# Row-tiled attention scores, early sums weighed later, whole-tile weight splits and a new issue plan in a fused attention, mixture-of-experts and squared-ReLU kernel

## The chip, the cores and the metric

One NeuronCore of a Trainium2 chip runs the whole kernel. The metric is device time in microseconds for one execution; a kernel is judged by the median of several runs. Beside them one execution was recorded by the profiler; its rows are what is read below. The engines are TensorE (PE for matmuls, PEld for the loads of their stationary operand), VectorE (DVE), ScalarE (ACT), GpSimd (POOL) and SyncE (SP), which issues most of the transfers.

## The reference

Three stages, all in f32 at the interface, on 4 batches of 576 positions, 8 heads of 64:

```python
# 1 attention with a causal window of 128 and a linear bias per head
scores = scale * q @ k.T            # per head
scores = where(0 <= rel < 128, scores - slope[h] * rel, -1e9)
attn = exp(scores - max); attn = attn / (sum + 1e-9);  x = attn @ v   # 2304 x 512
# 2 eight experts, every token to every expert, weights P by 8 row/column scalings
P = exp(x @ w_gate - max); 8 times: rows to 1, columns to 1, P *= N / E
out = sum over e of P[:, e] * (relu(x @ w1[e]) @ w2[e])               # 512 -> 1024 -> 512
# 3 squared ReLU layer
y = (relu(out @ w_in) ** 2) @ w_out                                   # 512 -> 2048 -> 512
```

## The kernel before

**Products.** The layers of stages 2 and 3 are done in 40 runs (e, b): experts e = 0 to 7 by batches b, then the two halves of the last layer (e = 8 and 9) by batches. Every operand is held as a high and a low f16 part and every product is three matmuls (THREE, L39). Each 2 x 2 block product is a seven-product scheme (m1 to m7, L44), so operands need sums of quarters and results are sums of products. A run is 336 matmuls of 128 x 128 by 288 columns: 168 for the hidden layer (`hidden`), 168 for the second one (`layer`). ScalarE or VectorE evict each product from PSUM into a quarter of a tile q (`to_quarter`), and cast hidden values to high and low (`split`).

**Attention.** 16 pairs of heads (two heads a and a + 1 on the two halves of the partitions), four units u of 128 queries each. `score_ops` (L856) writes the scores of a unit for both heads into one PSUM bank: a bf16 matmul of the identity by the bias tile first, then matmuls of Q by K onto it. For the first two batches (WHOLE = 2) Q is an f32 tile in which the other head's half is zero, so that a matmul contracts over 128 partitions. For the others `make_heads` (L823) casts Q and K to high and low f16 parts. `unit` (L881) takes the maxima from PSUM (VectorE), scales them, takes exp with its sum (ScalarE), scales by the reciprocal, transposes on TensorE and moves the result. `values` multiplies by V in f32. `take_x` and `take_sums` make the operands x of the batch, and expert 0 starts on a batch as soon as these are there, so attention of later batches and runs of expert 0 share the engines.

**Gate and early sums.** P needs all four batches, so runs that end before P is known (EARLY, five of them) are written to DRAM as they are (`spill`). `weigh` (L1146) starts when P is there: it brings each one back, multiplies by P (`by_p`, VectorE) and writes or adds it to acc_s in DRAM. A later run's sum q may be added (`y_next`, L1181) only when its batch has been weighed. `convert` (L1268) turns the last layer's 32 weight pieces, which come as 64-bit floats, to f32 and f16 parts, from the end of the weighing on, in the order of all of win and then wout. `retake` and `operands` read acc_s back and make the last layer's operands.

**Weights.** `Weights.make` (L563) splits a staged tile of 128 x 1024 in two halves k, each in a piece of 3 quarters ahead of the sums (`combine_w`) and one of 4 behind.

**What sets the order.** The program is written out by a planner (`Sched`) when it is built. Each chain of work is a thread; the planner knows a modelled cost of every operation and of every transfer (BEGIN, moves, LANDS, STORED, ADDED), and issues next the operation whose modelled start, less a lead, is earliest. Leads are constants (LEAD_...) or grow as a due time counted in products comes near (`by`, L387, with SLOPE, FAR and MARGIN). Where two engines can do an operation (`either`, `move`) the prices in PRICE choose. On each engine, and on the queues that issue transfers, the order so written is kept; an engine waits at whatever is next.

Of the kernel before, what the change touches and what calls it, by code (L numbers as in the profile page):

```python
# [86 lines left out]
LEAD_ATT, LEAD_LOGIT, LEAD_W0, LEAD_GATE, LEAD_WEIGH = -0.2988, -0.1623, -0.5925, -0.2787, 0.2666  # L87
SLOPE, FAR = 0.0083, 35.3894
MARGIN = {'TAKE': 8.6326, 'TAKE2': 8.6184, 'SPLIT': 0.7677, 'ADD': 10.9442, 'W': 4.7897, 'CONV': -22.9922, 'RETAKE': -15.7173}

AGE = 0.206

PRICE = {'A': -0.074, 'D': 0.577, 'G': 0.181, 'GW': 0.465, 'GS': 0.613, 'DF': 0.694, 'DR': 0.417, 'DM': 0.123, 'DN': 0.55, 'DX': 0.486, 'AS': -0.04, 'T': 0.0, 'S': 0.0}

SPARE = 6
WHOLE = 2


FRONT = dict(zip("PQRSTX", (((0,), 1), ((1,), 1), ((2,), 1), ((0, 1, 3, 4), 4), ((2, 5, 6), 3), ((7,), 1))))
MIDDLE = dict(zip("PQRSTX", (((0,), 1), ((1,), 1), ((2,), 1), ((3, 4), 2), ((5, 6), 2), ((7,), 1))))  # L100
# [9 lines left out]
RATE = {"A": 0.83e-3, "D": 1.04e-3, "G": 2.1e-3}  # L110
# [4 lines left out]
BEGIN, LANDS, STORED, ADDED = 0.65, 1.15, 0.35, 3.2  # L115
# [5 lines left out]
class Op:  # L121


    def __init__(self, engine, cost, reads, writes, issue, moves=0.0, lands=0.0, double=False):
        self.engine, self.cost, self.reads, self.writes, self.issue, self.moves, self.lands = engine, cost, reads, writes, issue, moves, lands
        self.price = PRICE[engine]

        self.port = engine == "G" or (engine == "D" and (double or sum(a.space != PSUM and a.free_size() > 8 for a in reads) > 1))
# [81 lines left out]
class Sched:  # L210
# [5 lines left out]
    def __init__(self):  # L216
        self.free = dict.fromkeys("TADGS", 0.0)
        self.port = self.moved = 0.0
        self.warm = 6.0
        self.place, self.marks, self.threads, self.count = {}, {}, [], 0  # L220
# [27 lines left out]
    def issue(self, op, start):  # L248
        op.issue()
# [29 lines left out]
    def run(self, until=None):  # L279
        while self.threads:  # L280
# [14 lines left out]
            for th in self.threads:  # L295
# [8 lines left out]
                key = (start - th.lead() if callable(th.lead) else start - th.lead - AGE * (start - ready), th.order)  # L304
# [40 lines left out]
def attn_moe_relu2(ctx: ExitStack, tc: tile.TileContext, qT, kT, v, wg, w1, w2, win, wout, bias, out):  # L345
# [12 lines left out]
    identb = const.tile([128, 128], BF16, name="identb")  # L358
# [27 lines left out]

    def by(due, kind):  # L387

        margin = MARGIN[kind]
        return lambda: -SLOPE * min(FAR, max(-5.0, (due - state["products"]) * PRODUCT + margin))  # L390
# [43 lines left out]
    def ts(out, in0, s, op, s2=None, op2=None):  # L434
# [4 lines left out]
            "D", START["D"] + RATE["D"] * size(out) / (2 if fast else 1) + 0.06 * (len(reads) - 1), reads, [out],  # L439
            lambda: nc.vector.tensor_scalar(out, in0, s, s2, op0=op, **k), double=fast,  # L440
        )

    def stt(out, in0, s, in1, op0, op1):
        return Op(
            "D", START["D"] + RATE["D"] * size(out), [in0, in1], [out],
            lambda: nc.vector.scalar_tensor_tensor(out=out, in0=in0, scalar=s, in1=in1, op0=op0, op1=op1),  # L446
        )
# [20 lines left out]
    def mms(seq):  # L468

        cost, reads, writes = 0.0, [], []  # L470
        for o, l, r, _, _ in seq:
            n = size(o)
            cost += 0.0025 + (n / 1200 if r is None else (4 * max(n, 112) if r.dtype == F32 else max(n, 44)) / 2400)
# [30 lines left out]
    def dma(out, in_):  # L504
        m = moves(out, in_)
        return Op("S", 0.46, [in_], [out], lambda: nc.sync.dma_start(out=out, in_=in_), m, STORED if out.space == DRAM else LANDS)
# [25 lines left out]
    def priced(kind, op):  # L532
        op.price = PRICE[kind]
# [4 lines left out]
    class Weights:  # L538
# [24 lines left out]
        def make(self, kind, c, t):  # L563
# [13 lines left out]
    def products(operands, known, banks, take, order, base, due, end):  # L577
# [14 lines left out]
        for step, (m, i0, i1) in enumerate(order):  # L592
# [15 lines left out]
            state["products"] += len(seq)  # L608
            if i1 == n:
# [157 lines left out]
    state = {"logits": 0, "wgs": False, "att": False, "gate": False, "weigh": False, "run": 0, "products": 0}  # L767

    with tc.manual_schedule():
        make_identity(nc, ident)  # L770
        nc.vector.tensor_copy(identb, ident)
        nc.vector.memset(ones, 1.0)

        with ExitStack() as actx:
            apool = lambda name, bufs, **k: actx.enter_context(tc.tile_pool(name=name, bufs=bufs, **k))
            ap = apool("ap", 1)
            r_qk = ring("qk32", ap, 3, [128, 2, S])
            r_kl = ring("kl", ap, 2, [128, 2, S], F16)
            r_b = ring("bia", ap, 2, [128, 512], BF16)
            r_e = ring("e", ap, RE, [128, 4, 2, 64])  # L780
            r_et = ring("eT", ap, 2, [128, 24, 64])
            qs = [ap.tile([128, 2, S], F32, name=f"q{i}") for i in range(2)]
            vs = [ap.tile([128, 9, 2, 64], F32, name=f"v{i}") for i in range(2)]

            for t in qs:
                nc.gpsimd.memset(t[64:128, 0], 0.0)
                nc.gpsimd.memset(t[0:64, 1], 0.0)
# [3 lines left out]
            r_q2, r_v = Kept(qs), Kept(vs)  # L791
            r_xq = ring("xq", ap, RX, [128, 4, HT])
            r_nm = ring("nm", ap, RE, [128, 4])
            r_sm = ring("sm", ap, RE, [128, 4])

            pairs = [(b, p) for b in range(B) for p in (0, 2, 1, 3)]
            qk32, qk, bias_in, values_in, eT, scored, moved = {}, {}, {}, {}, {}, {}, {}

            def load_heads():
                for n, (b, p) in enumerate(pairs):  # L800
                    h = slice(2 * p, 2 * p + 2)
                    if b < WHOLE:
                        Q = yield Need(r_q2)
                        for a in range(2):
                            yield dma(Q[64 * a : 64 * a + 64, a], qT[b, 2 * p + a])
                        K = yield Need(r_qk)
                        yield dma(K[:, 0], kT[b, h].rearrange("h d s -> (h d) s"))
                        qk[b, p] = (Q, K), ((r_q2, Q), (r_qk, K))
                    else:
                        t = []  # L810
                        for src in (qT, kT):
                            x = yield Need(r_qk)
                            for i in range(2):
                                yield dma(x[64 * i : 64 * i + 64], src[b, h].rearrange("h d s -> d h s"))
                            t.append(x)
                        qk32[b, p] = t
# [3 lines left out]
                    if n == 0:  # L820
                        spawn(load_values(), LEAD_ATT)

            def make_heads():  # L823


                for at in pairs[NP * WHOLE :]:
                    yield lambda: at in qk32
                    q32, k32 = qk32.pop(at)
                    t = yield Need(r_q2)
                    x = t.rearrange("p a s -> p (a s)").bitcast(F16).rearrange("p (i a s) -> p i a s", i=2, a=2)  # L830
                    Q, KH = x[:, 0], x[:, 1]
                    KL = yield Need(r_kl)
                    yield act(Q, q32)
                    yield either(Q[64:128], q32[64:128], Q[64:128], ALU.subtract)
                    r_qk.free(q32)
                    yield act(KH, k32)
                    yield either(KL, k32, KH, ALU.subtract)
                    r_qk.free(k32)
                    qk[at] = (Q, KH, KL), ((r_q2, t), (r_kl, KL))

# [15 lines left out]
            def score_ops(at, u, ps):  # L856
                full = lambda x: x.rearrange("p (a c) -> p a c", a=2)
                f, t = full(ps), full(bias_in[at])
# [552 lines left out]
```

## Time and profile before

| | us |
|---|---|
| runs | 1883.63, 1877.82, 1883.71 (median 1883.63) |
| profiled execution, its own time | 1878.17 |
| its span | 1876.4 |
| PE busy | 1814.9 (97%) |
| PEld busy | 1445.2 (77%) |
| DVE busy | 1576.8 (84%) |
| ACT busy | 1244.3 (66%) |
| POOL busy | 169.3 (9%) |

The span is the part of the profiled execution in which instructions ran. Busy time of PE includes the modelled ends of pipelined matmuls, so neighbouring groups overlap, and the distance from one group's start to the next one's is the better measure of what a group takes. The transfers take a mean of 136 GB/s, with stretches of 253 GB/s (about 420 to 470 us) and 273 GB/s (about 1500 to 1550 us).

### The profile page before, as it was taken

To read this page: it belongs to the slowest core of one execution; us is meant where nothing else is said; L and a number is where in the kernel's file an instruction comes from. 1 tells how busy PE (TensorE), PEld (TensorE's weight loads), DVE (VectorE), ACT (ScalarE), POOL (GpSimd) and SP (SyncE) were. 2 spreads that over 40 slices of the span, in tenths; PEclk is the share of its full clock that TensorE was granted. 3 is DMA by queue.
4 is the path that set the end of the run, shared out by engine and by line. 5 is a ranking of instruction groups with operands and counts; after the bars stand their busy time and mean duration, and the time that the engine had idled before them with its cause. 6 is when DMAs were issued, how large, how long until landed. Compare 5 with 4: busy or idle time off the path is not lost.

```text
span 1876.4 us, 38768 instructions
## 1 busy us (share of the span) xinstructions
PE 1814.9 (97%) x15077; PEld 1445.2 (77%) x15077; DVE 1576.8 (84%) x3475; ACT 1244.3 (66%) x3217; POOL 169.3 (9%) x207
## 2 busy tenths in 40 slices
PE   8899999898999999999999999999999999999999
PEld 7778777686777777777777777777777777777777
DVE  7987778897799999999999999999867777666666
ACT  7998876665566666666666667666646566666555
POOL 1110001100101212110012111111000000000000
PEclk9999999998999999999999999999999999999999
DMA  6554412438655535444453555345445585121321
GB/s 164 168 141 109 138 52 74 134 117 253 178 149 151 155 101 159 141 120 118 149 162 93 149 163 164 94 133 147 112 161 146 156 273 178 70 110 63 128 102 70
DMA packets 88233, 255.44 MB, mean 136 GB/s; under 512 B 26992, under 2 KB 35312, under 8 KB 88048
## 3 DMA queue, kind: packets, MB, share of 16 engines
q1 hardware_dynamic: 79984, 219.93, 35.2%
q0 software_dynamic: 8064, 33.03, 9.9%
q8 instruction: 118, 1.93, 0.4%
q14 instruction: 67, 0.55, 0.1%
HBM read 168.57 MB, written 84.35 MB: 135 GB/s over the span
## 4 chain that ended last, share of the span: by engine, by line
PE 60%; DVE 20%; DMA 8%; ACT 7%; issue 4%; SPq 0%; POOL 0%; DVEq 0%; ACTq 0%; POOLq 0%
PE ps L482 60%; DVE h L431 5%; DVE q L431 4%; DVE t L431 3%; ACT q L414 2%; DVE w L446 2%; DMA acc_s<-q 2%; DMA wst<-in_w 2%; DMA x_s<-wo 2%; ACT h L414 1%; ACT e L414 1%; DVE wz L431 1%; DVE wo L446 1%; ACT w L414 1%; DMA yw<-y_s 1%
## 5 line engine op out<-in xcount | busy, mean ns | idle before, releaser
L482 PEld LDWEIGHTS <-w 128*128 128x128 f16 x13440 | 1315.7, 98 | 395.9 <-issue 65.0
L482 PE MATMUL ps<-x,w 128*128 128x288 f16 x6720 | 861.2, 286 | 32.9 <-ACT q L414 19.1
L482 PE MATMUL ps<-h,w 128*128 128x288 f16 x6720 | 857.4, 286 | 14.4 <-DVE q L431 5.8
L414 ACT ACTIVATE q<-ps 128x288 f32<-128x288 f32 x926 | 364.5, 403 | 279.6 <-PE ps L482 268.6
L431 DVE TENSOR_TENSOR q<-ps,q 128x288 f32<-128x288 f32 x672 | 291.5, 449 | 106.5 <-PE ps L482 85.4
L414 ACT ACTIVATE q<-q 128x288 f32<-128x288 f32 x411 | 174.9, 440 | 95.2 <-DVE q L431 93.3
L414 ACT ACTIVATE h<-t 128x576 f16<-128x576 f32 x320 | 212.6, 679 | 30.8 <-DVE t L431 28.3
L414 ACT ACTIVATE h<-q 128x288 f16<-128x288 f32 x480 | 203.8, 439 | 4.4
L414 ACT ACTIVATE w<-wst 128x384 f16<-128x384 f32 (+1 forms) x256 | 141.1, 572 | 80.0 <-DMA wst<-in_w 38.0
L431 DVE TENSOR_TENSOR h<-q,h 128x288 f16<-128x288 f32 x384 | 173.3, 465 | 24.2 <-ACT h L414 23.3
L431 DVE TENSOR_TENSOR h<-t,h 128x576 f16<-128x576 f32 x256 | 188.5, 754 | 1.8 <-ACT h L414 0.9
L446 DVE SCALAR_TENSOR_TENSOR w<-wst,w 128x384 f16<-128x384 f32 (+1 forms) x256 | 161.4, 638 | 8.7 <-ACT w L414 8.4
L431 POOL TENSOR_TENSOR wst<-wst 128x256 f32<-128x256 f32 x107 | 97.1, 909 | 585.4 <-DVE wst L431 334.0
L431 DVE TENSOR_TENSOR t<-q,t 128x288 f32<-128x288 f32 x315 | 140.5, 456 | 1.9 <-ACT q L414 1.0
L431 DVE TENSOR_TENSOR t<-q 128x576 f32<-128x576 f32 x160 | 122.8, 770 | 6.2 <-ACT q L414 4.0
L431 DVE TENSOR_TENSOR q<-q,pb 128x576 f32<-128x576 f32 x108 | 83.6, 784 | 6.3 <-ACT q L414 5.6
L510 POOL DMA_DIRECT2D acc_s<-q x54 | 47.5, 907 | 431.2 <-DVE q L431 404.8
L414 ACT ACTIVATE e<-ps,nm 128x192 f32<-128x192 f32 (+1 forms) x160 | 64.1, 410 | 15.7 <-DVE nm L440 12.7
L431 DVE TENSOR_TENSOR wst<-wst 128x256 f32<-128x256 f32 x149 | 61.8, 426 | 2.4 <-POOL wst L431 0.5
L414 ACT ACTIVATE wo<-wz 128x384 f16<-128x384 f32 x64 | 36.8, 574 | 38.4 <-DVE wz L431 17.7
L453 DVE TENSOR_REDUCE nm<-ps 128x2 f32<-128x384 f32 (+1 forms) x80 | 38.3, 495 | 18.7 <-PE ps L482 18.4
L446 DVE SCALAR_TENSOR_TENSOR h<-q,h 128x288 f16<-128x288 f32 x96 | 43.1, 450 | 12.6 <-ACT h L414 12.6
(94 smaller groups left out, 1059.3 us busy)
## 6 DMA issues: line engine op xcount, KB each, us to landing
x<-x_s SPq DMA_DIRECT2D x56, 1008.0 KB, 4.8
wst<-in_w SPq DMA_DIRECT2D x64, 512.0 KB, 4.7
acc_s<-q POOLq DMA_DIRECT2D x54, 576.0 KB, 6.8
pb<-p_s SPq DMA_DIRECT2D x32, 288.0 KB, 5.5
yw<-in_win SPq DMA_DIRECT2D x16, 512.0 KB, 5.4
yw<-in_wout SPq DMA_DIRECT2D x16, 512.0 KB, 4.9
x_s<-x SPq DMA_DIRECT2D x8, 1008.0 KB, 4.9
win_s<-wo SPq DMA_DIRECT2D x16, 448.0 KB, 3.1
```

Of the source, the lines that this page charges most:

```text
L414: return Op("A", cost, reads, writes, lambda: nc.scalar.activation(out=out, in_=in_, func=func, scale=scale, **k))
L431: lambda: engine(e).tensor_tensor(out=out, in0=in0, in1=in1, op=op),
L446: lambda: nc.vector.scalar_tensor_tensor(out=out, in0=in0, scalar=s, in1=in1, op0=op0, op1=op1),
L453: lambda: nc.vector.tensor_reduce(out=out, in_=in_, axis=axis, op=op, **k),
L482: nc.tensor.matmul(o, l, r, start=start, stop=stop, skip_group_check=True)
L510: return Op("G", 1.04, [in_, out], [out], lambda: nc.gpsimd.dma_start(out=out, in_=in_, accum_op=ALU.add), m, ADDED)
```

## The change

- **Scores.** All pairs are f32 and unpadded. Each score matmul contracts over the 64 partitions of one head, and the two heads alternate, each into a PSUM bank of its own; two units at a time share the two banks (`two` takes the place of `unit`; `make_heads`, the padded Q, the identity in bf16 and the bias matmuls go). The bias is added by VectorE while it takes the score from PSUM into e, with the minimum of the scaled sum kept beside (`add_min`); exp then reads e. Scaling e by the reciprocal may also go to GpSimd. Q and K come in one transfer each, the first K issued from ScalarE's queue.
- **Running array.** Until the first expert run starts, `fill` issues matmuls of a constant tile into an own PSUM bank wherever the planner sees TensorE free, each counted as 0.216 us.
- **Early sums.** EARLY has six runs. Whichever term of acc_s comes first is written, the others are added (`give`), in any order of runs. `weigh` takes the n-th tile at 336 (8 + 2 n) products.
- **Weights and conversion.** `Weights.make` splits both halves k in one instruction each. `convert` squares on ScalarE where VectorE masked a sign, is due over runs 13 to 35, and does the first half of win and wout first.
- **Plan.** LEAD, MARGIN, SLOPE, AGE and PRICE become entries of PLAN that change at 1000, 1900, 6000 and 9400 products. Landing times and GpSimd's rate are raised. PSUM banks of the front are dealt out anew; the second half of a batch in `operands` uses the ring of staged weights.

```diff
-LEAD_ATT, LEAD_LOGIT, LEAD_W0, LEAD_GATE, LEAD_WEIGH = -0.2988, -0.1623, -0.5925, -0.2787, 0.2666
-SLOPE, FAR = 0.0083, 35.3894
...
+PLAN = [
+    (0, {
+        "ATT": -0.2046, "LOGIT": -0.3502, "W0": -0.4909, "GATE": 0.3571, "CAST": -0.315, "SLOPE": 0.015925,
...
-FRONT = dict(zip("PQRSTX", (((0,), 1), ((1,), 1), ((2,), 1), ((0, 1, 3, 4), 4), ((2, 5, 6), 3), ((7,), 1))))
+FRONT = dict(zip("PQRST", (((0,), 1), ((1,), 1), ((2,), 1), ((2, 5, 6, 7), 4), ((0, 3, 4), 3))))
...
-RE, RX = 5, 1
-
-EARLY = [(0, b) for b in range(B)] + [(1, B - 1)]
+RE, RX = 3, 2
+WEIGH = (8, 2)
+CONVERT = (13.028, 22.236)
+EARLY = [(0, b) for b in range(B)] + [(1, B - 1), (1, B - 2)]
...
-RATE = {"A": 0.83e-3, "D": 1.04e-3, "G": 2.1e-3}
+RATE = {"A": 0.83e-3, "D": 1.04e-3, "G": 2.55e-3}
...
-BEGIN, LANDS, STORED, ADDED = 0.65, 1.15, 0.35, 3.2
+BEGIN, LANDS, STORED, ADDED = 0.65, 2.63, 0.81, 3.80
+FILL = 0.216
...
+        if op.engine == "T" and self.fill:
+            one = FILL * (2 if start < self.warm else 1)
+            n = int((start - self.free["T"] - 0.1) / one)
+            if n > 0:
+                self.fill(n)
+                self.free["T"] = start
...
+    def add_min(out, least, in0, in1, scale):
+        return Op(
+            "D", START["D"] + 0.06 + RATE["D"] * size(out), [in0, in1], [out, least],
+            lambda: nc.vector.tensor_tensor_reduce(
+                out=out, in0=in0, in1=in1, scale=scale, scalar=3.0e38, op0=ALU.add, op1=ALU.min, accum_out=least
+            ),
         )
...
-            for k in range(2):
-                yield from split(dst[:, k, 0, 0:3], dst[:, k, 1, 0:3], st[:, k, 0:3], SW)
+            yield from split(dst[:, :, 0, 0:3], dst[:, :, 1, 0:3], st[:, :, 0:3], SW)
             yield from combine_w(st)
-            for k in range(2):
-                yield from split(dst[:, k, 0, 3:], dst[:, k, 1, 3:], st[:, k], SW)
+            yield from split(dst[:, :, 0, 3:], dst[:, :, 1, 3:], st, SW)
...
+                    for p0, n, c0, w_, q0, k0 in parts:
+                        for a in range(2):
+                            r = slice(64 * a, 64 * a + 64)
+                            c = 256 * j + c0
+                            seq.append((ps[a][p0 : p0 + n, c : c + w_], Q[r, q0 : q0 + n], K[r, k0 : k0 + w_], True, True))
+                return mms(seq, together=2)
...
+                for i in range(m + 1):
+                    if i < m:
+                        n, a, j, s = each[i]
...
+                        yield add_min(e[:, j, s, a], nm[:, n : n + 1], f[:, s], t[:, at_bias, a], -ISQ)
+                    if i:
+                        n, a, j, s = each[i - 1]
+                        yield act(e[:, j, s, a], e[:, j, s, a], AF.Exp, -1.0, nm[:, n : n + 1], sm[:, n : n + 1])
...
+        def give(b, j, y):
+            if (b, j) in begun:
+                return dma_add(acc_s[b][j], y)
+            begun.add((b, j))
+            return dma(acc_s[b][j], y)
...
-                    yield lambda: len(p) and b in weighed and got >= ({"m2", "m3"} if d == 0 else {"m7", "m4"})
+                    yield lambda: len(p) and got >= ({"m2", "m3"} if d == 0 else {"m7", "m4"})
...
-            for i in range(32):
+            for i in (*range(8), *range(16, 24), *range(8, 16), *range(24, 32)):
...
-                yield ts(z, hi, 0x7FFFFFFF, ALU.bitwise_and)
-                yield stt(hi.bitcast(F32), zf, 3.4332275390625e-05, hi.bitcast(F32), ALU.is_ge, ALU.mult)
+                yield act(zf, hi.bitcast(F32), AF.Square)
+                yield stt(hi.bitcast(F32), zf, 3.4332275390625e-05**2, hi.bitcast(F32), ALU.is_ge, ALU.mult)
...
-            o = yield Need(r_wo, [128, 2, 3, HT])
+            r = r_wst if k else r_wo
+            o = yield Need(r, [128, 2, 3, HT], F16)
```

## Rows read from the trace of the kernel before

**Rows 1.** Windows: from:to, length, busy (count) of PE, PEld, DVE, ACT, POOL, clock, DMA.
```profile
0.00:376.00 376.00, 348.00 (x3226) 284.10 (x3227) 312.26 (x821) 302.58 (x909) 36.79 (x48) 1.00 0.43 122
...
47.00:94.00 47.00, 42.09 (x409) 35.95 (x409) 43.63 (x121) 43.14 (x140) 7.16 (x8) 1.00 0.59 169
...
440.00:480.00 40.00, 31.23 (x222) 23.02 (x221) 27.75 (x55) 15.47 (x37) 0.87 (x1) 0.87 0.85 271
750.00:1320.00 570.00, 560.39 (x4544) 444.11 (x4543) 541.26 (x1131) 375.06 (x912) 75.05 (x91) 1.00 0.47 136
```

**Rows 2.** Windows, PE only, matmuls that read a weight tile w.
```profile
0.00:376.00 376.00, 212.14 (x1597) 1.00 0.43 122
440.00:480.00 40.00, 31.23 (x222) 0.87 0.85 271
750.00:1320.00 570.00, 560.39 (x4544) 1.00 0.47 136
1500.00:1600.00 100.00, 94.69 (x748) 0.98 0.63 214
1600.00:1700.00 100.00, 100.00 (x816) 1.00 0.23 84
```

**Rows 3.** Timeline of PE: start, length, group; f32 units, then fp16 units.
```profile
28.49 0.33 PE L482 MATMUL ps<-bia,identb 128*128 128x384 bf16 x1
28.75 1.10 PE L482 MATMUL ps<-qk,q 128*64 128x64 f32 x12
29.68 0.38 PE L482 MATMUL ps<-bia,identb 128*128 128x128 bf16 x2
...
31.00 1.25 PE L480 MATMUL ps<-ident,e 128*128 128x128 f32 x10
...
163.19 0.33 PE L482 MATMUL ps<-bia,identb 128*128 128x384 bf16 x1
...
163.93 0.38 PE L482 MATMUL ps<-bia,identb 128*128 128x128 bf16 x2
...
164.60 0.90 PE L482 MATMUL ps<-x,w 128*128 128x288 f16 x6
```

**Rows 4.** Timeline of PE at the start and after the early sums; idle before in brackets.
```profile
6.96 2.34 PE L482 MATMUL ps<-qk,q 128*128 128x64 f32 x8
...
448.26 1.60 PE L482 MATMUL ps<-x,w 128*128 128x288 f16 x6 [5.35 <-ACT q L414]
```

**Rows 5.** Groups of instructions: busy us, mean ns of one, idle before and its releaser.
```profile
L482 PE MATMUL ps<-wgs,x 128*128 128x8 f16 x80 | 5.1, 166 | 0.0
...
L414 ACT ACTIVATE q<-qk 128x1152 f16<-128x1152 f32 x16 | 18.6, 1162 | 0.4 <-PE ps L482 0.4
L431 DVE TENSOR_TENSOR kl<-qk,q 128x1152 f16<-128x1152 f32 x8 | 10.8, 1351 | 0.1
L453 DVE TENSOR_REDUCE nm<-ps 128x2 f32<-128x384 f32 x64 | 35.0, 547 | 7.7 <-PE ps L482 7.5
L440 DVE TENSOR_SCALAR nm<-nm 128x2 f32<-128x2 f32 x48 | 8.4, 174 | 0.6
L414 ACT ACTIVATION_READ_ACCUMULATOR e<-ps,nm 128x1 f32 x160 | 34.8, 217 | 0.0
...
L431 DVE TENSOR_TENSOR q<-ps,q 128x288 f32<-128x288 f32 x672 | 291.5, 449 | 106.5 <-PE ps L482 85.4
L446 DVE SCALAR_TENSOR_TENSOR w<-wst,w 128x512 f16<-128x512 f32 x128 | 90.4, 711 | 2.6 <-ACT w L414 2.3
L446 DVE SCALAR_TENSOR_TENSOR w<-wst,w 128x384 f16<-128x384 f32 x128 | 71.7, 566 | 6.1 <-ACT w L414 6.1
L440 DVE TENSOR_SCALAR wz<-yw 128x512 uint32<-128x512 uint32 x64 | 28.6, 446 | 4.2 <-DMA yw<-in_win 2.0 <-DMA yw<-in_wout 1.8
L431 DVE TENSOR_TENSOR yw<-yw,pb 128x576 f32<-128x576 f32 x20 | 14.1, 752 | 3.6 <-DMA yw<-y_s 3.5
```

**Rows 6.** Transfers: issues of one line, KB each, median us from issue to landing.
```profile
wst<-in_w SPq DMA_DIRECT2D x64, 512.0 KB, 4.7
```

More of the change, by code (lines that the diff above doesn't have):

```diff
@@ L303, in run @@
                     )
[L304 removed]
+                key = (start - th.lead() if callable(th.lead) else start - th.lead - K["AGE"] * (start - ready), th.order)
                 if best is None or key < best[0]:
@@ L385, in attn_moe_relu2, with plan @@
     r_wst = ring("wst", main, 2, [128, 1024])
+    def plan():
+        while steps and state["products"] >= steps[0][0]:
+            K.update(steps.pop(0)[1])
     def by(due, kind):
-        margin = MARGIN[kind]
-        return lambda: -SLOPE * min(FAR, max(-5.0, (due - state["products"]) * PRODUCT + margin))
+        return lambda: -K["SLOPE"] * min(K["FAR"], max(-5.0, (due - state["products"]) * PRODUCT + K[kind]))
     def size(ap):
@@ L766, in attn_moe_relu2 @@
     converted = set()
-    state = {"logits": 0, "wgs": False, "att": False, "gate": False, "weigh": False, "run": 0, "products": 0}
+    steps = list(PLAN)
+    state = {"logits": 0, "wgs": False, "att": False, "gate": False, "cast": False, "run": 0, "products": 0}
+    plan()
     with tc.manual_schedule():
         make_identity(nc, ident)
-        nc.vector.tensor_copy(identb, ident)
         nc.vector.memset(ones, 1.0)
@@ L776, in attn_moe_relu2, with fill @@
             ap = apool("ap", 1)
[L777 to L780, printed above, removed]
+            run = ap.tile([128, 512], BF16, name="run")
+            nc.vector.memset(run, 1.0)
+            idle = bank["Q"].take(None, None)
+            def fill(n):
+                for _ in range(n):
+                    nc.tensor.matmul(idle, run[:, 0:128], run, start=True, stop=True, skip_group_check=True)
+            sched.fill = fill
+            r_qk = ring("qk", ap, 6, [128, S])
+            r_b = ring("bia", ap, 3, [128, 512], BF16)
+            r_e = ring("e", ap, RE, [128, 2, 4, 2, 64])
             r_et = ring("eT", ap, 2, [128, 24, 64])
-            qs = [ap.tile([128, 2, S], F32, name=f"q{i}") for i in range(2)]
             vs = [ap.tile([128, 9, 2, 64], F32, name=f"v{i}") for i in range(2)]
-            for t in qs:
-                nc.gpsimd.memset(t[64:128, 0], 0.0)
-                nc.gpsimd.memset(t[0:64, 1], 0.0)
             for t in vs:
@@ L801, in load_heads @@
                     h = slice(2 * p, 2 * p + 2)
[L802 to L816, printed above, removed]
+                    t = []
+                    for i, src in enumerate((qT, kT)):
+                        x = yield Need(r_qk)
+                        yield dma(x, src[b, h].rearrange("h d s -> (h d) s"), "A" if n == 0 and i else "S")
+                        t.append(x)
+                    qk[b, p] = t
                     t = yield Need(r_b)
@@ L820, in load_heads @@
                     if n == 0:
[L821 to L839, printed above, removed]
+                        spawn(load_values(), K["ATT"])
             def load_values():
@@ L942, in values @@
                     xs = []
-                    for r_, part in zip((bank["X"], bank["T"]), parts):
-                        x = yield Need(r_)
+                    for part in parts:
+                        x = yield Need(bank["T"])
                         xs.append(x)
@@ L1038, in take_runs @@
                         yield lambda: b in make_x
+                        if sched.fill:
+                            sched.fill = None
+                            bank["Q"].free(idle)
                         for k, n in MIDDLE.items():
@@ L1113, in sinkhorn @@
                 ps = yield Need(bank["S"])
-                yield mms([(ps[:, 0:E], ones, cs, True, True)])
+                yield from cast([(ps[:, 0:E], ones, cs, True, True)])
                 ci = small.tile([128, 1, E], F32, tag="ci", name="ci")
@@ L1301, in retake @@
             for b in reversed(range(B)):
-                yield lambda: added.get((E - 1, b)) == 2 and all(eb in early_added for eb in y_s if eb[0] and eb[1] == b)
+                yield lambda: all(added.get((e, b)) == 2 for e in range(E))
                 for k in range(2):
```

239 lines of the change are left out of this document (130 added, 109 removed), and 3 rows, old and new, of the table PLAN.

## The prediction

> **What bounds the kernel now.** I read the windows of all engines first. From 0 to 376 us, where attention runs beside the first expert runs, TensorE is busy 348.0 of 376 us, ScalarE 302.6, VectorE 312.3; from 750 to 1320 us TensorE is busy 560.4 of 570 and VectorE 541.3, 95% [rows 1]. So TensorE sets the pace, and VectorE is the engine that nearly ties with it. Then the same windows cut to the matmuls that read a weight tile w. In 1600 to 1700 us TensorE does 816 of them in 100 us without a gap, 122.55 ns each; at that price each stretch tells how long it lasted beyond its products [rows 2]. From 0 to 376: 376 − 1597 × 0.12255 = 180 us. From 440 to 480: 40 − 27.2 = 12.8 us, with the granted clock at 0.87. From 750 to 1320: 570 − 556.9 = 13.1 us. From 1500 to 1600: 100 − 91.7 = 8.3 us. The products themselves, 40 × 336 × 0.12255 = 1647 us, are untouched by the change; all that it can win lies in the 229 us around them, four fifths of it in the front. There 348.0 − 212.1 = 136 us of TensorE is attention and 28 us is idleness, nearly 7 us of that before the first scores at 6.96 us [rows 1, 2, 4].
>
> **The change part by part.**
>
> *Scores on TensorE.* The timeline of PE shows the issue distance of each score group. An f32 unit with u = 1 to 3 takes 29.68 − 28.49 = 1.19 us, 0.26 of it the bias matmul; u = 0 takes 31.00 − 29.68 = 1.32, its bias taken alike. Per pair 3 × 1.19 + 1.32 = 4.89 us, for the 8 pairs of the first two batches 39.1 us [rows 3]. An fp16 unit takes 163.93 − 163.19 = 0.74 us, u = 0 takes 164.60 − 163.93 = 0.67: 2.89 per pair, 23.1 us for the other 8. Together 62.2 us. After the change all 16 pairs are f32 without bias matmuls: in a row, 3 × 0.93 + 1.06 = 3.85 per pair, 61.6 us; if the two heads' halves of the array run side by side, 30.8 us. No row shows half-array matmuls, nor what it costs to change between halves and the whole. For that I bound: nothing at the low end, and at the high end the 166 ns of one lone 8-column matmul, whose time is nearly all filling and emptying [rows 5], at 64 changes (32 groups, in and out), 10.6 us. Side by side with changes paid: 62.2 − 30.8 − 10.6 = 20.8 us less. I take −20; the ends are −31 and +10 (a row of full-length groups, changes paid).
>
> The Trainium skill (TensorEngine Tiling (Array Packing), Theoretical Speedup and Key Properties) puts two row tiles at up to twice the speed, and says that changing the tiling mode drains TensorE. By its first sentence alone the term would be −31, with the drain it is the −20 taken; no trace of the kernel before shows either.
>
> *Is that on the path?* In the front TensorE is busy 93% against 83% of VectorE and 80% of ScalarE [rows 1], so TensorE work left out counts if the other two shed as much. ScalarE loses the 16 casts of Q and K to f16, 18.6 us; VectorE the 10.8 us of K's low parts and about as much for Q's, the 64 long maxima of 35.0 us (some short ones beside), and 64 scalings of nm at 174 ns, 11.1 us: 67.7 in all [rows 5]. VectorE gains 160 add_min (128 of 192 columns, 32 of 64), an operation that no row shows. The nearest row adds from PSUM: 449 ns for 288 columns; with 1.13 ns a column from the two w rows, (711 − 566)/128, that is 340 and 196 ns, 49.8 us [rows 5]. The upper end: two passes a column and a separate accumulator read of 217 ns as ScalarE's (34.7 us more), 134 us. The lower end: no fixed cost, 1.13 ns a column, 30 us. I take 49.8, since that row shares its operands' places. VectorE's front then falls from 312 to 294 and ScalarE's from 303 to 284: both shrink about as TensorE does (348 to 328), so −20 stays on the path. Of the 21 us of TensorE idleness behind the start I take 4 back, for looser neighbours and a third score buffer less in the way of fp16 copies; ends −12 and +10 (units of two hold two PSUM banks each, so only two groups are in flight, and one that waits for its exp blocks the next).
>
> The Trainium skill (VectorE: DVE Perf Modes, Two Vector instructions with no wait between them) says that an operation that also writes out its accumulator is two instructions. At ScalarE's read price it would turn VectorE's −18 into +17 us; no row here shows it for VectorE.
>
> *Start.* The first scores stand at 6.96 us behind the first bias matmul, which needs the bias tile, and that group takes 2.34 us where the same records later take 1.06 and their bias 0.26 [rows 3, 4]. Now no bias is needed to start TensorE, Q comes in one transfer, and K is issued from ScalarE's queue beside it. The dummy matmuls fill planned gaps of TensorE until the first expert run. They stand in the in-order queue, so a real group that is ready early waits for what is left of them; their number comes from the plan's gaps, so I count them as free (end: +5). I take −3, ends −5 and +5.
>
> *Early sums.* At 448.26 us TensorE has waited 5.35 us for ScalarE, and the 6 matmuls behind take 1.60 us where 6 at 122.55 ns are 0.74, at a granted clock of 0.87 over the stretch [rows 1, 4]. DMA is busy 0.85 there: ten spilled tiles come back in a burst, q buffers are held until their batch has been weighed, and ScalarE has no q to evict into. The change takes away both: any term may be the first in acc_s, so no q waits for another batch, and the burst becomes 12 tiles spread over runs 8 to 18. A sixth spilled run also puts off the first need of the gate by 336 × 0.1225 = 41 us. The work moves under VectorE at 95%: 24 multiplications of 752 ns [rows 5], 18 us, against 20 before. I take −10, ends −12.8 and +5 (18 us on a full VectorE, a quarter of it seen). On POOL the adds are as many as before: each half of a batch still takes eight sums, the first of them written plain.
>
> *Runs.* Weights split whole: per tile two pairs of VectorE instructions become one each; 566 + 566 becomes 566 + 384 × 1.13 = 1000 ns and 711 + 711 becomes 1290, 0.26 us per tile, 17 us over 64, as much or less on ScalarE. The conversion passes one of its VectorE steps of 446 ns to ScalarE: 32 × 0.446 = 14 us [rows 5]; ScalarE has 195 us idle in 750 to 1320, so there it is covered. Converting from run 13 to 35 instead of 9 to 27 carries a part past 1320, where VectorE is looser. The planner's landing time is the other half: its BEGIN + transfer + LANDS for a weight tile is 0.65 + 1.27 + 1.15 = 3.1 us, the trace shows 4.7 [rows 6]; with LANDS 2.63 it is 4.6, so an order is no longer laid out for tiles that are 1.6 us late. For 13.1 us of loss I take −5, ends −10 and +6 (VectorE instructions of 1.3 us stand longer before an eviction).
>
> *Before the last layer.* The two halves of a batch are cast out of different rings, not one after the other. Of 8.3 us I take −3, ends −8 and +5.
>
> **Sum.** −20 − 4 − 3 − 10 − 5 − 3 = −45, made against the profiled execution's 1878.17 us (span 1876.4): 1833. The three runs shown lie at 1877.82 to 1883.71 with the median 5.5 us above the profile; the runs of the changed kernel may lie on either level, so I put 2 on it: 1835 us. With all low ends 1800; with weak ones in each term about 1865.
>
> **Rivals.**
> 1. *The halves don't overlap.* Scores cost 61.6 + 10.6 us: +10 in place of −20, the rest as above: 1835 + 30 = 1865. For it: no row shows overlap. Against: the two heads write separate PSUM banks and read separate partitions.
> 2. *The pace of the front is set by ScalarE and VectorE.* TensorE's −20 and −4 turn into its own idleness: 1859. For it: from 47 to 94 us VectorE is busy 43.6 and ScalarE 43.1 of 47 us, 93 and 92%, more than TensorE's 42.1 [rows 1]; against: both shed 18 us.
> 3. *Slower: add_min.* Two passes and a read, 134 us, put VectorE's front at 312 − 68 + 134 = 378 us, more than the stretch. At the 93% of 47 to 94 us that is 406 us, 30 more than now; with the other four terms 1878 + 30 − 3 − 10 − 5 − 3 + 2 = 1889. It decides from 397 us of front on (21 more eat the other four terms): (397 × 0.93 − 244)/160, about 0.78 us a piece against 0.31 taken.
>
> **How the numbers follow.** Forecast 0.64 (its own range 1805 to 1862), rival 1 0.14, rival 2 0.08, rival 3 0.14. About 0.3%, 5.6 us, is what a measurement here can tell from nothing. Faster: 0.63 + 0.11 + 0.06 = 0.80; the same: 0.01 + 0.03 + 0.02 + 0.02 = 0.08; slower: 0.12, all of rival 3. The range is 1798 to 1882: below it is only a sum of nearly all low ends (0.07), above it rival 3 (0.12).
>
> **What would show it.** Score records of the two heads that start within tens of ns of each other and a group of 12 records in about 0.5 us: step one right; 0.93 us or a gap at each change: rival 1. add_min near 340 ns for 192 columns, and no read behind it: VectorE's term. The first matmul with data before 5 us. No stretch behind the front with a clock under 0.95, and no wait of 5 us for ScalarE. Excess in 750 to 1320 us under 9 us. The prediction is wrong if the front's excess over its products stays above 165 us, or if a new stretch in runs 8 to 18 or before run 36 loses over 10 us, because the moved weighing or the later conversion arrives late.

## The result, and the profile after

The changed kernel takes 1820.19 us (1819.69 to 1821.09, 4 runs) against 1882.58 us before (1877.82 to 1883.71): a ratio of 0.9674, 95% interval 0.9656 to 0.9692. The forecast was 1835 us. The profiled execution took 1821.09 us, its span is 1819.2, so the spans differ by 57.2 us where the sum had 45.

First the page's busy times of the changed kernel, then its windows of all engines and those cut to the matmuls that read a weight tile w (columns as in [rows 1, 2]).

```profile
PE 1795.8 (99%) x15028; PEld 1433.4 (79%) x15031; DVE 1557.0 (86%) x3519; ACT 1204.0 (66%) x2994; POOL 137.1 (8%) x173
```

```profile
0.00:376.00 376.00, 362.19 (x3358) 292.26 (x3362) 308.34 (x924) 291.35 (x850) 43.64 (x55) 0.99 0.38 122
376.00:480.00 104.00, 103.85 (x844) 81.86 (x842) 96.51 (x235) 66.10 (x158) 4.19 (x7) 1.00 0.28 99
480.00:1264.00 784.00, 783.16 (x6388) 624.73 (x6386) 710.14 (x1427) 518.29 (x1197) 70.39 (x89) 1.00 0.52 146
```

```profile
0.00:376.00 376.00, 233.05 (x1790) 0.99 0.38 122
376.00:480.00 104.00, 102.31 (x824) 1.00 0.28 99
480.00:1264.00 784.00, 783.16 (x6388) 1.00 0.52 146
1444.00:1544.00 100.00, 98.33 (x800) 1.00 0.71 243
```

The kernel before, asked for the same two later stretches:

```profile
376.00:480.00 104.00, 95.23 (x740) 0.95 0.61 198
480.00:1264.00 784.00, 771.44 (x6252) 1.00 0.49 138
```

A stretch's length less 0.12255 us for each product in it is its loss, as in the prediction. The last line of the table is what is left of each span (13440 products taken off), and the line above it is the rest, since a product on a border counts in both stretches. The forecast for 480 to 1264 us is the prediction's term for 750 to 1320.

| stretch, us | loss before | loss after | measured | forecast |
|---|---|---|---|---|
| 0 to 376 | 180.3 | 156.6 | −23.7 | −27 |
| 376 to 480 | 13.3 | 3.0 | −10.3 | −10 |
| 480 to 1264 | 17.8 | 1.2 | −16.6 | −5 |
| 1264 to the end | 17.9 | 11.3 | −6.6 | −3 |
| whole span | 229.3 | 172.1 | −57.2 | −45 |

In 480 to 1264 TensorE now stops for under 1 us. The front holds 193 more products in the same 376 us, and VectorE's busy time there falls only from 312 to 308 us: it does the evictions and casts of these products (97 sums with a product from PSUM where it did 84) and 12 us of the conversion, while 14 us of the gate's scalings are no longer in this stretch.

### The profile page after: what moved, and what is told of

Read it like the earlier page. It is cut to its first block, busy times and chain, and to the rows that moved or that the text cites. A ratio compares the mean times of both kernels' runs of the same rounds, so it can differ in the third digit from the quotient of the medians.

```text
span 1819.2 us, 38389 instructions
## 1 busy us (share of the span) xinstructions
PE 1795.8 (99%) x15028; PEld 1433.4 (79%) x15031; DVE 1557.0 (86%) x3519; ACT 1204.0 (66%) x2994; POOL 137.1 (8%) x173
## 4 chain that ended last, share of the span: by engine, by line
PE 84%; DVE 8%; ACT 4%; DMA 3%; issue 1%; SPq 0%; ACTq 0%; DVEq 0%
PE ps L541 82%; DVE t L480 2%; DVE q L480 1%; DVE h L480 1%; DVE h L495 1%; DMA acc_s<-q 1%; PE ps L539 1%; ACT h L463 1%; ACT q L463 1%; ACT e L463 1%; DMA yw<-in_wout 1%; DMA acc_s<-yw 1%; PE ps L843 1%; DVE w L495 0%; DMA x_s<-wst 0%
## 5 line engine op out<-in xcount | busy, mean ns | idle before, releaser
L463 ACT ACTIVATE q<-q 128x288 f32<-128x288 f32 x389 | 167.4, 440 | 78.0 <-DVE q L480 76.6
L463 ACT ACTIVATE w<-wst 128x768 f16<-128x768 f32 (+1 forms) x128 | 120.1, 944 | 63.1 <-DVE wst L480 41.4
L495 DVE SCALAR_TENSOR_TENSOR w<-wst,w 128x1024 f16<-128x1024 f32 (+1 forms) x128 | 139.1, 1091 | 3.5 <-ACT w L463 3.0
L480 POOL TENSOR_TENSOR wst<-wst 128x256 f32<-128x256 f32 x65 | 57.1, 882 | 384.0 <-DVE w L495 197.9
L480 DVE TENSOR_TENSOR q<-q,pb 128x576 f32<-128x576 f32 x104 | 77.1, 750 | 3.7 <-ACT q L463 3.0
L480 DVE TENSOR_TENSOR wst<-wst 128x256 f32<-128x256 f32 x191 | 77.9, 421 | 1.9
L570 POOL DMA_DIRECT2D acc_s<-q x46 | 40.1, 872 | 519.8 <-DVE q L480 472.6
L463 ACT ACTIVATE e<-e,nm 128x192 f32<-128x192 f32 (+1 forms) x160 | 67.7, 425 | 16.0 <-DVE nm L502 15.8
L502 DVE CUSTOM_DVE_ANT_0 e<-ps,bia 128x192 f32<-128x192 f32 (+1 forms) x160 | 46.9, 322 | 23.6 <-PE ps L541 17.8
L541 PE MATMUL ps<-eT,v 128*128 128x192 f32 (+2 forms) x384 | 54.5, 293 | 0.8 <-ACT eT L463 0.7
```

What stands on the lines that cost most here:

```text
L463: return Op("A", cost, reads, writes, lambda: nc.scalar.activation(out=out, in_=in_, func=func, scale=scale, **k))
L480: lambda: engine(e).tensor_tensor(out=out, in0=in0, in1=in1, op=op),
L502: lambda: nc.vector.tensor_tensor_reduce(out=out, in0=in0, in1=in1, scale=scale, scalar=3.0e38, op0=ALU.add, op1=ALU.min, accum_out=least),
L541: nc.tensor.matmul(o, l, r, start=start, stop=stop, skip_group_check=True)
L570: return Op("G", 1.04, [in_, out], [out], lambda: nc.gpsimd.dma_start(out=out, in_=in_, accum_op=ALU.add), m, ADDED)
```

## The experiments

Each kernel was timed in rounds beside the kernel before; where a ratio is given it is to that one. The runs a1 to a4 and c1 keep the changed kernel's issue order and alter only what an entry of it holds; b1 to b4 and c2 let the planner write a new order; c3 and c4 put one part of the change into the kernel before, in an order planned anew.

**a1_serial.** Is it the overlap of the two heads that shortens the scores?

```diff
+                n = len(seq)
+                seq = seq[0:n:2] + seq[1:n:2]
                 return mms(seq, together=2)
```

> The issue order of every engine stays as in the changed kernel; only inside a score group all matmuls of the first head now come before those of the second, so two neighbouring matmuls use the same half of the array. Theory (the halves overlap): the groups grow from 1.45 and 1.39 us (20 and 24 records) by what one head's part takes, to about 2.0 and 1.9 us, 1.0 us a pair, 16 us over 16 pairs, and most of it reaches the end: 1831 to 1837 us. Rival (the groups are short because a contraction over 64 partitions is itself cheaper, not because the heads overlap): groups unchanged, 1820 us.

1868.56 us (1864.03 to 1873.12), ratio 0.9936 [0.9912, 0.9961]: 48 us of the gain are gone. PE timelines, of the changed kernel, then of a1_serial:

```profile
160.92 1.46 PE L541 MATMUL ps<-qk 64*64 64x64 f32 x24
162.31 1.64 PE L541 MATMUL ps<-x,w 128*128 128x288 f16 x12
...
169.79 1.52 PE L541 MATMUL ps<-qk 64*128 64x64 f32 x20
171.24 0.55 PE L539 MATMUL ps<-ident,e 128*128 128x128 f32 x3
```

```profile
144.09 2.78 PE L541 MATMUL ps<-qk 64*64 64x64 f32 x24
146.80 2.08 PE L541 MATMUL ps<-eT,v 128*128 128x64 f32 x14
...
152.19 2.50 PE L541 MATMUL ps<-qk 64*128 64x64 f32 x20
154.62 0.91 PE L541 MATMUL ps<-h,w 128*128 128x288 f16 x6
```

From start to start, units 2 and 3 (24 records) go from 1.39 to 2.71 us and units 0 and 1 (20 records) from 1.45 to 2.43: 2.30 us a pair, 37 us over 16. The rival (no overlap) is out. But the expected growth was 1.0 us a pair, and the next run shows what the rest is. The other 11 us are what is left over; a lower clock stands beside them: from 10 to 30 us the granted clock is 0.57 where the changed kernel has 1.00, with TensorE as busy in both. How much of the 11 us it makes was not measured by itself. First a1_serial, then the changed kernel:

```profile
10.00:30.00 20.00, 19.45 (x94) 12.71 (x96) 8.12 (x46) 10.49 (x40) 0.77 (x1) 0.57 0.46 131
```

```profile
10.00:30.00 20.00, 19.45 (x199) 15.14 (x204) 18.54 (x94) 19.33 (x74) 4.45 (x6) 1.00 0.62 181
```

**a2_sorted.** What does a change of the tile's shape cost inside a group?

```diff
+                seq.sort(key=lambda x: -x[1].free_size())
                 return mms(seq, together=2)
```

> Same issue order, only inside a score group the matmuls with 128 stationary columns come before those with 64. In the changed kernel's trace the weight loads of a group pause 0.23 us where 128 columns change to 64. Theory (a change of the tile's shape empties TensorE): the group of units 2 and 3 changes shape once instead of three times and gets 0.3 to 0.5 us shorter, 5 to 8 us over 16 pairs, 1813 to 1817 us. Rival (the pause is only the first load of a group that waits): groups unchanged, 1820 us.

1812.12 us (1811.94 to 1812.62), ratio 0.9634 [0.9611, 0.9657]: 8 us faster than the changed kernel, the fastest of all kernels here. Its PE timeline:

```profile
140.72 1.11 PE L541 MATMUL ps<-qk 64*128 64x128 f32 x24
141.76 0.91 PE L541 MATMUL ps<-x,w 128*128 128x288 f16 x6
...
147.76 1.31 PE L541 MATMUL ps<-qk 64*128 64x64 f32 x20
149.01 2.38 PE L541 MATMUL ps<-x,w 128*128 128x288 f16 x18
```

24 records now take 1.04 us instead of 1.39 with one change of shape instead of three, 20 records 1.25 instead of 1.45 with one instead of two: 0.18 and 0.20 us a change, and 0.55 us a pair, 8.8 us over 16. In a1_serial the groups have four and two changes more than in the changed kernel; taken off at these prices, 2.71 and 2.43 become 2.0 and 2.0 us. So of the 2.3 us a pair, about 1.1 were shape changes and 1.2 the overlap, 18 and 19 us over 16 pairs.

**a3_nofill.** What do the dummy matmuls earn?

```diff
-            sched.fill = fill
+            sched.fill = lambda n: None
```

> Same issue order without the dummy matmuls. Theory (18 dummies before the first scores, 0.43 us each at 1.2 GHz, hold TensorE until 8.14 us although Q and K land at about 5 us): the first scores start near 5 us, and the front ends 1 to 3 us sooner: 1817 to 1819 us. Rival (the dummies earn more by having the clock at 2.4 GHz when the scores come): the first groups take twice as long, nothing gained, 1820 to 1823 us.

1819.70 us (1818.76 to 1820.75): nothing. PE timelines of the changed kernel and of a3_nofill:

```profile
1.59 6.62 PE L843 MATMUL ps<-run 128*128 128x512 bf16 x18 [1.59 <-DVE run L838]
...
8.14 2.91 PE L541 MATMUL ps<-qk 64*128 64x64 f32 x44
```

```profile
4.75 5.19 PE L541 MATMUL ps<-qk 64*128 64x64 f32 x46 [4.75 <-DMA qk<-in_kT]
```

The dummies hold TensorE for 3.4 us after the data have landed (4.75 us). Without them the same two groups and a bit take 5.19 instead of 2.91 us, and the next two groups end at 15.2 us instead of 14.8. The windows put the granted clock at 1.00 from 0 to 10 us in both, so they do not show why the groups are slower. The two come out even, between the two expectations.

**c1_best.** Both: the sorted groups, and fewer dummies.

```diff
-                for _ in range(n):
+                for _ in range(min(n, 8)):
...
+                seq.sort(key=lambda x: -x[1].free_size())
```

> The changed kernel with the score matmuls of 128 columns ahead of those of 64 (alone: 1812.1 us) and at most 8 dummy matmuls in one gap, the issue order of all else unchanged. Theory (18 dummies at the start hold the first scores back by 3 us, and none at all leaves them at half clock, which came out even): 8 end at about 5 us, when the data land, with the clock nearly up: 1809 to 1811 us. Rival (the front is paced by ScalarE and VectorE there, not by TensorE's start): 1812 us.

1813.13 us (1812.11 to 1815.85): no gain over a2_sorted, though the first scores stand at 5.11 us, where a2_sorted has them at 7.42 and the changed kernel at 8.14. The rival held: in both kernels TensorE then stands 3.73 us for ScalarE's x, and from 30 to 40 us ScalarE and VectorE are busy 8.9 and 9.8 of 10 us, TensorE 6.3. The head start is 1.5 us behind that wait and 0.1 us at the score group of 24 records at 58 us (57.81 against 57.93). What part of it went with the clock, 0.70 in these ten us against 0.83 in a2_sorted, is not shown. PE timelines of c1_best and of a2_sorted, then windows of c1_best:

```profile
5.11 3.11 PE L541 MATMUL ps<-qk 64*128 64x64 f32 x44
...
34.21 1.77 PE L539 MATMUL ps<-ident,e 128*128 128x128 f32 x6 [3.73 <-ACT x L463]
```

```profile
7.42 2.35 PE L541 MATMUL ps<-qk 64*128 64x64 f32 x44
...
35.76 0.59 PE L539 MATMUL ps<-ident,e 128*128 128x128 f32 x3 [3.73 <-ACT x L463]
```

```profile
30.00:40.00 10.00, 6.25 (x27) 5.40 (x29) 9.77 (x36) 8.87 (x29) 1.96 (x1) 0.70 0.70 218
```

**a4_halves.** Did VectorE's shorter weight work take the runs' waits away?

```diff
+    def halves(hi, lo, src):            # same place in the order, two instructions
+        for one in split(hi, lo, src, SW):
+            parts = [list(split(hi[:, k], lo[:, k], src[:, k], SW))[0 if one.engine == "A" else 1] for k in range(2)]
...
-            yield from split(dst[:, :, 0, 0:3], dst[:, :, 1, 0:3], st[:, :, 0:3], SW)
+            yield from halves(dst[:, :, 0, 0:3], dst[:, :, 1, 0:3], st[:, :, 0:3])
...
```

> Same issue order, but every split of a weight tile is written as two instructions of half the length again on ScalarE and VectorE. VectorE gets back about 0.26 us a tile, 17 us in all, ScalarE somewhat more. Theory (the runs lose less mainly because the plan spreads the work, and VectorE at 91% has room): 1820 to 1825 us. Rival (VectorE's shorter work is what took the runs' waits away): the stretch from 750 to 1264 us loses 8 us or more again, 1828 to 1835 us.

1823.90 us (1821.56 to 1824.45): 3.7 us slower, little more than the runs of one kernel differ by. The runs from 610 to 1264 us lose no more than without the edit; what is lost lies ahead of 480 us, 3.3 us of it in the front, where ScalarE and VectorE set the pace in places. Theory right.

**b1_null.** What may a replanned order differ by?

```diff
-        "FAR": 16.7394, "AGE": 0.229, ...
+        "FAR": 16.7394, "AGE": 0.235, ...
```

> The changed kernel with one planning constant moved by 3% (AGE of the first stretch from 0.229 to 0.235): nothing of the work changes, but the planner writes another order from the front on. It gives the size that any replanned run may differ by without a cause. Theory (the order follows the modelled times and is robust): 1817 to 1826 us. Rival (the constants fit this one order, and its waits are what was won): 1830 us or more.

1828.26 us (1827.47 to 1828.94): 8 us, just outside the theory's 1817 to 1826 and short of the rival's 1830. Most of it lies in 94 to 188 us; from 480 to 1264 us it loses 2.6 us where the changed kernel loses 1.2. By this one step, differences under about 8 us between replanned kernels name no cause by themselves; the place of a loss can.

**b2_lands.** The landing times of before.

```diff
-BEGIN, LANDS, STORED, ADDED = 0.65, 2.63, 0.81, 3.80
+BEGIN, LANDS, STORED, ADDED = 0.65, 1.15, 0.35, 3.2
```

> The changed kernel with the landing times of before in the planner (LANDS 1.15, STORED 0.35, ADDED 3.2). Theory (the wider times take waits away, which the weight tile's 4.7 us against a modelled 3.1 speaks for): TensorE waits for operands that come late, 1826 to 1840 us, with the loss spread over the runs. Rival (with two staged weight tiles the transfers are early enough anyway): within the replanned run's spread, 1817 to 1826 us.

1838.55 us (1837.64 to 1844.50): 18 us slower, inside the theory's range, but not spread over the runs: 1444 to 1544 us, before the last layer, loses 100 − 717 × 0.12255 = 12.1 us where the changed kernel loses 2.0, and the other 8 us are within what a replanning moves. Windows of b2_lands, matmuls that read w:

```profile
1444.00:1544.00 100.00, 91.39 (x717) 0.97 0.75 250
```

**b3_burst.** All early sums back as soon as the gate is there.

```diff
-WEIGH = (8, 2)
+WEIGH = (0, 0)
```

> The changed kernel, but all early sums may be taken back as soon as the gate is there, as before the change (WEIGH 0, 0), while no q waits for another batch. Theory (the burst of transfers and VectorE work lost the 13 us from 376 to 480 us): 5 to 12 us come back in the stretch behind the gate, 1825 to 1832 us. Rival (what lost them was that a q buffer had to wait until its batch was weighed): no loss there, 1818 to 1824 us.

1831.85 us (1831.41 to 1836.26), inside the theory's range. The loss is where the burst is: 130 − 981 × 0.12255 = 9.8 us in 480 to 610, with transfers busy 0.68. Windows of b3_burst, matmuls that read w:

```profile
480.00:610.00 130.00, 122.27 (x981) 0.99 0.68 194
```

**c4_before_give.** The other half of that step alone, in the kernel before: whichever term comes first is written, no q waits for a weighing.

```diff
...
-                    yield lambda: len(p) and b in weighed and got >= ...
+                    yield lambda: len(p) and got >= ...
...
-                        yield dma_add(acc_s[b][j], y)
+                        yield give(b, j, y)
...
```

> The kernel before with one part of the change alone: whichever term of acc_s comes first is written and no q waits until its batch is weighed; the early sums still come back in one burst. Theory (the burst itself, transfers at 85% and VectorE, makes half of the 13 us lost from 376 to 480 us): 4 to 8 us less, 1872 to 1877 us. Rival (the wait of q for the weighing was all of it): 10 to 13 us less, 1867 to 1871 us.

1877.77 us (1874.13 to 1881.16), ratio 0.9971 [0.9956, 0.9986]: 5.5 us less. The stretch loses 104 − 793 × 0.12255 = 6.8 instead of 13.3 us: half the wait, half the burst, as the theory had it. That rests on the place; 5.5 us in all is less than a replanning can move. Windows of c4_before_give, matmuls that read w:

```profile
376.00:480.00 104.00, 99.55 (x793) 0.98 0.60 197
```

**b4_convlate.** The conversion where it was before.

```diff
-CONVERT = (13.028, 22.236)
+CONVERT = (9, 18)
...
+            yield lambda: state["products"] >= 336 * 7
             for i in (*range(8), *range(16, 24), *range(8, 16), *range(24, 32)):
```

> The changed kernel, but the conversion of the last layer's weights starts after 7 runs and is due over runs 9 to 27, about where it ran before the change (its first piece stood at 511 us, the last at 1276; in the changed kernel 276 and 1574). Theory (spreading the conversion over 1300 us is what freed VectorE in the runs): VectorE is back at 94 to 96% from 750 to 1264 us, and that stretch loses 6 to 12 us: 1826 to 1833 us. Rival (the lighter work of VectorE and the plan are enough): 1818 to 1824 us.

1864.82 us (1863.56 to 1869.11): 45 us slower, far over the theory's 6 to 12. From 480 to 1264 us it loses 784 − 5988 × 0.12255 = 50.2 us instead of 1.2. TensorE stands still for 32.8 us of them; its waits there are 23.0 us for VectorE and 9.2 for ScalarE, most of them for evictions (us in total, times, longest). The other 17 us are no waits: it is busy 751.2 us with products worth 733.8, at a granted clock of 0.98. VectorE is at 93% there against 91%, not back at 94 to 96%, so it is not its sum of work. Nor is it shown that evictions stand right behind conversion pieces in its queue: of the 23 us in which TensorE waits for VectorE, about 4 are conversion pieces. In the longest wait VectorE works off hidden values (h) ahead of the eviction. That the pieces made its queue late further back is likely, and not shown. The windows of b4_convlate, matmuls that read w, its waits from 480 to 1264 us, and VectorE's timeline in the longest one, the 3.42 us up to 737.19:

```profile
480.00:1264.00 784.00, 751.22 (x5988) 0.98 0.55 153
```

```profile
PE ps L541 <- DVE q L480: 19.6, 22, 3.4
PE ps L541 <- ACT q L463: 9.2, 8, 3.0
PE ps L541 <- DVE h L480: 3.4, 5, 1.2
```

```profile
733.57 0.75 DVE L480 TENSOR_TENSOR h<-t,h 128x576 f16<-128x576 f32 x1
...
734.61 1.42 DVE L480 TENSOR_TENSOR h<-t,h 128x576 f16<-128x576 f32 x2
...
736.68 0.45 DVE L480 TENSOR_TENSOR q<-ps,q 128x288 f32<-128x288 f32 x1
```

**c3_before_conv.** The earlier, spread conversion alone, in the kernel before.

```diff
-            yield lambda: state["weigh"]
-            for i in range(32):
+            for i in (*range(8), *range(16, 24), *range(8, 16), *range(24, 32)):
...
-        spawn(convert(), lambda: by(336 * (9 + 18 / 32 * len(converted)), "CONV")())
+        spawn(convert(), lambda: by(336 * (13.028 + 22.236 / 32 * len(converted)), "CONV")())
```

> The kernel before with one part of the change alone: the conversion of the last layer's weights no longer waits for the weighing, takes the first halves of both weights first and is due over runs 13 to 35. Theory (spreading it frees VectorE in the runs, whose loss beyond the products was 17 us from 480 to 1320): that loss falls to under 8 us, and the time to 1865 to 1875 us. Rival (without the lighter VectorE work and the new plan the waits only move): 1878 to 1886 us.

1875.16 us (1873.40 to 1879.34), ratio 0.9968 [0.9957, 0.9979]: 8 us less, just past the theory's range, no more than a replanning can move, and not by its mechanism: 480 to 1264 us still loses 784 − 6260 × 0.12255 = 16.8 us against 17.8, though VectorE is at 91% there as in the changed kernel. Windows of c3_before_conv, matmuls that read w:

```profile
480.00:1264.00 784.00, 772.12 (x6260) 1.00 0.47 131
```

**c2_oldplan.** The changed kernel's work, planned with the constants of before.

```diff
-PLAN = [(0, {"ATT": -0.2046, "LOGIT": -0.3502, "W0": -0.4909, "GATE": 0.3571, "CAST": -0.315, ...}), (1000, ...
+PLAN = [(0, {"ATT": -0.2988, "LOGIT": -0.1623, "W0": -0.5925, "GATE": -0.2787, "CAST": -0.2787, ...})]
```

> The changed kernel's work, planned with the constants of before in one stretch (lead of the weighing and the prices that are new keep their values). A replanned run with a 3% step in one constant lost 8 us. Theory (the work and its due times are the gain, the constants fit it finely): 1826 to 1845 us, its loss spread over front and layer changes. Rival (the plan by stretches is most of the gain): 1850 us or more.

1904.70 us (1903.57 to 1911.09), ratio 1.0134 [1.0110, 1.0157]: slower than before, in the rival's range, but not as it was meant. Of the 84 us that it is behind the changed kernel, 61 are in one stretch: 130 − 554 × 0.12255 = 62.1 us lost from 480 to 610 us, against 1.2. So the time tells of the gate's place in the order, and little of the rest. There the gate's column sums stand in TensorE's queue, and TensorE waits 5 to 6 us at each of six for VectorE's sum cs, at a granted clock of 0.76. Windows of c2_oldplan, matmuls that read w, and its PE timeline:

```profile
480.00:610.00 130.00, 75.11 (x554) 0.76 0.47 149
```

```profile
505.51 0.60 PE L514 MATMUL ps<-cs,ones 128*128 128x8 f32 x2 [5.50 <-DVE cs L484]
...
518.34 0.59 PE L514 MATMUL ps<-cs,ones 128*128 128x8 f32 x2 [6.05 <-DVE cs L484]
```

In the changed kernel the same 16 records stand from 393 to 417 us with products between them, and their waits come to 1.6 us.

## Why the prediction was right, and where its terms were off

**The direction and the place** were right: TensorE sets the end, and what went is loss around unchanged products. The forecast missed by 15 us in the median and by 12 in the spans, 11.6 of these in one term.

**Runs, −5 against −16.6: the mis-sized term.** Its sign came out for reasons other than most of those given. VectorE's shorter weight work takes nothing from the runs in this order (a4), and the landing times take 1.4 us there (b2). What counts is the third, where the conversion runs. The prediction read its due times, runs 13 to 35, as the time when it runs. The edit also took away its wait for the weighing, and so it starts in the front. Summaries of the conversion's first step, of the changed kernel (first and last start at the end of the line), then of the kernel before:

```profile
L463 ACT ACTIVATE wz<-yw x32: 657/670/698, 275.9 to 1567.5; 128x512 f32<-128x512 f32 x32
```

```profile
L440 DVE TENSOR_SCALAR wz<-yw x64: 404/419/956, 510.6 to 1270.6; 128x512 uint32<-128x512 uint32 x64
```

Put late and dense again it costs 45 us in the new plan (b4). In the old plan it matters far less: dense, the runs lose 17.8 us, spread 16.8 (c3), with 5 us more lost from 480 to 610 us and 6 less behind. Windows from 610 us on, matmuls that read w, of the kernel before, of c3_before_conv, of c2_oldplan and of the changed kernel:

```profile
610.00:1264.00 654.00, 642.48 (x5203) 1.00 0.48 136
```

```profile
610.00:1264.00 654.00, 647.27 (x5253) 1.00 0.45 125
```

```profile
610.00:1264.00 654.00, 647.83 (x5263) 1.00 0.50 141
```

```profile
610.00:1264.00 654.00, 653.96 (x5339) 1.00 0.51 142
```

They lose 16.4, 10.2, 9.0 and nothing. So the spread is needed and not enough: with the constants of before, even all of the changed work leaves 9 us lost here (c2, whose gate came late), and with those of PLAN none is; a small step in one of them moves this stretch by 1 us only (b1 loses 0.9). How the whole term divides stays open, since each of these orders is planned anew and one such step moves 8 us of the time (b1).

**Scores, −20 against −17.** From start to start a pair takes 1.39 + 1.45 = 2.84 us, 45.4 over 16, where 62.2 stood and 30.8 + 10.6 = 41.4 were forecast. The overlap is real (a1). The prediction charged 64 changes into and out of a group at 166 ns; it did not see the five changes of tile shape inside the two groups of a pair, 0.18 to 0.20 us each (a2), some 15 us. What a change into or out of a group costs no run measured by itself. The Trainium skill's sentence that changing the tiling mode drains TensorE (TensorEngine Tiling (Array Packing), Key Properties) holds here, at these prices, also for a change between 64 x 128 and 64 x 64; it gives no price.

**Rival 3, add_min.** The groups of the changed kernel, from 0 to 260 us:

```profile
L502 DVE CUSTOM_DVE_ANT_0 e<-ps,bia 128x192 f32<-128x192 f32 x128 | 41.5, 348 | 8.0 <-PE ps L539 4.4 <-PE ps L541 3.6
...
L463 ACT ACTIVATION_READ_ACCUMULATOR e<-e,nm 128x1 f32 x160 | 30.7, 192 | 0.0
...
L502 DVE DVE_READ_ACCUMULATOR2_ANT nm<- 128x1 f32 x160 | 13.0, 81 | 0.0
...
L502 DVE CUSTOM_DVE_ANT_0 e<-ps,bia 128x64 f32<-128x64 f32 x32 | 5.8, 219 | 15.5 <-PE ps L541 14.3 <-PE ps L539 1.1
```

348 and 219 ns stand against 340 and 196 taken, and there is a read behind each, as the Trainium skill has it (VectorE: DVE Perf Modes, Two Vector instructions with no wait between them): 81 ns, not ScalarE's 217 [rows 5], which is 192 here. That is 60 us in all, 10 more than the 49.8 taken and far from the 134 of the rival.

**Start, −3 against +1, and the idleness behind it, −4 against −5.** The first scores stand at 8.14 us, later than the 6.96 of [rows 4]: the dummies, costed at nothing, are what is late. It does not matter: neither removing them (a3) nor starting with 8 of the 18 (c1) moves the end, for ScalarE and VectorE pace the first 60 us. From 10 to 60 us they are busy 46.5 and 47.1 of 50 us, TensorE 42.6. That is rival 2 in a small part of the front; for the whole of it, it fell, since 8.8 us less of TensorE work gave 8.1 us of time in a2. Behind the start TensorE was idle 21 us; now it is idle or runs dummies for 16. Windows of the changed kernel, first all engines, then the dummies alone:

```profile
10.00:60.00 50.00, 42.61 (x403) 34.00 (x407) 47.09 (x193) 46.48 (x164) 12.85 (x14) 0.97 0.60 176
```

```profile
0.00:376.00 376.00, 10.41 (x31) 0.99 0.38 122
```

**Early sums, −10 against −10.3,** and by the two parts named: the wait of q (c4) and the burst (b3). **Before the last layer, −3 against −6.6 from 1264 us on:** with the landing times of before the new plan loses 10 us more there (b2), so they count here, where the prediction had put them under the runs. What the second ring for the operands earns no run separates.

**Weight splits, −17 us of VectorE**: worth 3.7 us at the end (a4), ahead of 480 us.

## What to carry to other kernels

Half-array matmuls paid here when their neighbours sat on different halves, and the order inside such a group should keep tile shapes together: sorting them brought 8 us where the tiling had brought 17. Where background work is put and how the rest is planned belong together: in the new plan the conversion lost 1.2 us in the runs when spread thin and 50.2 when dense, in the old one 16.8 and 17.8. Where an order is planned, a part of a change that is moved into another plan can cost more than it brings, so take the place of a loss, and not only the sum, as evidence.

## What the runs showed of the hardware that was not expected

- A change between 64 x 128 and 64 x 64 tiles cost TensorE 0.18 to 0.20 us inside groups of f32 score matmuls (1.39 us with three changes, 1.04 with one).
- The granted clock was 0.57 for 20 us, near the lower of its two levels (1.2 and 2.4 GHz), with TensorE busy 97% of them, when all its score matmuls used one half of the array after the other; with the halves side by side it was 1.00 at the same busy share. This is one profiled execution of each.
- VectorE's read of its accumulator took 81 ns, ScalarE's 192 in the same kernel.
